# Nystrom attention with a routed FFN on one core: the pseudo-inverse's second four heads in tiles of their own, the last four batches solved in pairs

## The chip, the core and the metric

The kernel runs on one core of one Trainium2 chip. The metric is device time in microseconds of one execution; three executions of the kernel before took 290.11, 291.2 and 293.77 us, median 291.2.

The engines are named as in the profile: PE is TensorE (matrix products; PEld are its weight loads), DVE is VectorE, ACT is ScalarE, POOL is GpSimd, and SP issues most DMAs.

## What is computed

Attention by landmarks for 8 batches, 8 heads, 576 rows, 64 columns, then a mixture of experts on its output. In short:

```python
q_lm = q.reshape(B, H, 32, 18, 64).mean(3)        # 32 landmarks a head; k_lm alike
A  = softmax(scale * q @ k_lm.T)                  # 576 x 32
Bm = softmax(scale * q_lm @ k_lm.T)               # 32 x 32
C  = softmax(scale * q_lm @ k.T)                  # 32 x 576
Z = Bm.T / (norm1(Bm) * norminf(Bm) + 1e-6)
for _ in range(6):
    Z = 2 * Z - Z @ Bm @ Z                        # the pseudo-inverse
x = A @ Z @ C @ v                                 # (4608, 512) when the heads stand side by side
e = argmax(x @ w_gate)                            # one of 8 experts a row
out = p_e * sigmoid(x @ w_output_gate)[e] * (relu(x @ w1[e]) @ w2[e])
```

w1 is 8 x 512 x 1024, w2 is 8 x 1024 x 512; p_e is the softmax of the gate at the chosen expert.

## The kernel before

One core does all 8 batches. A batch is two halves (`hf`) of four heads each; the four heads of a half stand in the four groups of 32 partitions.

*Attention of a half.* SP brings q, k and v. For batches 0 to 2 TensorE transposes q and k (L455), for the others VectorE does (L469). Landmark sums are made by VectorE (L481) or GpSimd (L483 to L487). The scores of C and A (L528) use 32 x 32 or 64 x 32 tiles of the array, where head h of the queries writes to column group h, and head h of the keys to column group h+2, so that both run in different tiles. C goes through its exponential (L550), a transpose (L558) and the product with v (L570) into `XW`, a tile that holds for each half 32 columns of B beside 64 columns of C v. A is softmaxed by VectorE, ScalarE and GpSimd (L587 to L608).

*B and the pseudo-inverse of a batch.* B's scores (L621), maximum (L627), exponential with sums (L633), normalising (L645 on ScalarE or L647 on VectorE), column sums by a product with ones (L655), their largest (L661 to L664), and the scaled negative `nx` (L670 or L672). Then comes a chain of seven steps (L685): each multiplies, for every one of the eight heads, a 32 x 32 matrix by the 32 x 96 columns of the current tile (the seventh by 64), into one PSUM bank, and two copies, one for each half, bring it back into a new tile `X` (L697; the last one is L709). Matmul of head h always uses row group h and column group h; the second half follows the first through the same four tiles. A step depends on the copies of the step before. In the trace one fp32 matmul is two instructions, so a step shows 16.

*Gate and routing.* A transpose (L715), the gate's product (L723), the logits (L734) and small work on VectorE (L753 to L796) choose one main expert for the batch; GpSimd then fetches its weights with DMAs (L364, L367), unless the batch two before had the same. x transposed is made by L816.

*FFN of a batch.* 16 `up` groups of four matmuls (L861), each followed by a relu on ScalarE or VectorE (L396, L402); then, for 5 row tiles, two `down` groups each (L878, L881), the scaling (L890, L892), and the DMA out (L902). Rows whose expert isn't the main one are handled after the loop, if there are any.

*Banks.* PSUM has two pairs of banks `S` and four banks `M`. Attention work may hold at most CAPA = 4 of the four M banks, the FFN CAPF = 3, or 4 from batch LASTF = 5 on.

*What sets the order.* No engine's order is written by hand. `Plan` collects the operations of all batches with their reads, writes, tiles, an assumed duration on each engine that can do it, and a priority (PR for attention of a batch, FR for its FFN). `Plan.run` then places one operation after another by the assumed times: the one that can begin first, or one of better priority that begins soon after (TOL, PAT, MARGIN), on the engine where it ends first, with a handicap (`shy`) for VectorE or GpSimd. For TensorE it adds SWITCH = 95 ns where the tile shape changes. The program that runs has the operations of each engine in the planned order, with semaphores for the dependencies; so a changed duration or priority changes the order everywhere.

Of the kernel before, what the change touches and what calls it, by code (L numbers as in the profile page):

```python
# [71 lines left out]
class Plan:  # L72
# [6 lines left out]
    PE_LAG = 185.0  # L79
    SWITCH = 95.0  # L80
# [4 lines left out]
    MARGIN = 0.2  # L85
    SHARE = 0.6
    TOL = 60.0
    PAT = 900.0
    PAT_PE = 150.0
# [48 lines left out]
    def run(self):  # L138
# [18 lines left out]
        while ready:  # L157
            cands = []
            for o in ready:
# [106 lines left out]
def kernel(  # L266
# [75 lines left out]
    t_AT = tag("AT", 4, [128, UP])  # L342
    t_XW = tag("XW", 2, [128, 2, m + D])
    t_X = tag("X", 4, [128, 2, m + D])
    t_sm = tag("sm", 8, [128, 64])
    t_co = tag("co", B, [128, NT])
    t_ZT = tag("ZT", 4, [128, 128])
    t_nx = tag("nx", 2, [128, 2, m])
    t_G = tag("G", 2, [128, 2, m])
    t_lg = tag("lg", 2, [128, NT, m])  # L350
    t_rt = tag("rt", 2, [128, 8, NT, E])
# [17 lines left out]
    with tc.manual_schedule():  # L369
# [37 lines left out]
        def evac(n):  # L407
            return {"ACT": 45 + 0.85 * n, "DVE": 30 + 1.08 * n}
# [10 lines left out]
        def batch(b):  # L419
            pr = PR[b]  # L420
            lms, ATs, sms, ZVp = [], [], [], []
            XW = Val(t_XW)
            P.op({"": 0}, lambda e: None, w=[XW["home"]], prio=pr)
            for hf in range(2):
# [81 lines left out]
                def l_of(lm, wide, x, h, j):  # L506
                    if wide:
                        return lm.t[j * D:(j + 1) * D, x, h * m:(h + 1) * m]
                    return lm.t[h * m:(h + 1) * m, 0, (2 * x + j) * m:(2 * x + j + 1) * m]

# [4 lines left out]
                sms.append(st)  # L515
# [63 lines left out]
                def pv_out(e, pV=pV, st=st, hf=hf):  # L579
                    if e == "ACT":  # L580
                        nc.scalar.activation(out=XW.t[:, hf, m:], in_=pV.t[:, :D], func=COPY, scale=st.t[:, 3:4])
                    else:
                        nc.vector.tensor_scalar(out=XW.t[:, hf, m:], in0=pV.t[:, :D], scalar1=st.t[:, 3:4],
                                                scalar2=None, op0=MUL)
                P.op({"ACT": 230, "DVE": 190}, pv_out, r=[pV[0], st[2]], w=[XW[f"y{hf}"]], shy={"DVE": SHYE}, prio=pr + .04)

# [25 lines left out]
            pr = PR[b] + 0.1  # L612
            pB = Val(p_M, "attn", CAPA)
            sb = Val(t_sm)

            def b_scores(e):
                for hf in range(2):
                    for h in range(HH):
                        r_ = slice(h * m, (h + 1) * m)
                        for j in range(1 if wide else 2):  # L620
                            nc.tensor.matmul(pB.t[r_, hf * m:(hf + 1) * m], lhsT=l_of(lms[hf], wide, 0, h, j),  # L621
                                             rhs=l_of(lms[hf], wide, 1, h, j), start=(j == 0), stop=(j == 1 or wide))
            P.op({"PE": 150 if wide else 250}, b_scores, recs=32 if wide else 64, r=[lms[0][0], lms[1][0]], w=[pB[0]], hold=[sb],
                 mode=(D, m) if wide else (m, m), prio=pr + .025)

            def b_max(e):
                nc.vector.tensor_reduce(sb.t[:, 0:2], pB.t[:, :2 * m].rearrange("p (a r) -> p a r", a=2), axis=X, op=MAX)  # L627
            P.op({"DVE": 130}, b_max, r=[pB[0]], w=[sb[0]], prio=pr + .025)

            def b_exp(e):  # L630
                nc.scalar.mul(sb.t[:, 2:4], sb.t[:, 0:2], -s_bm)
                for hf in range(2):
                    nc.scalar.activation(out=XW.t[:, hf, :m], in_=pB.t[:, hf * m:(hf + 1) * m], func=EXP, scale=s_bm,  # L633
                                         bias=sb.t[:, 2 + hf:3 + hf], accum_out=sb.t[:, 4 + hf:5 + hf])
            P.op({"ACT": 680}, b_exp, r=[pB[0], sb[0]], w=[XW["x0"], XW["x1"], sb[1]], prio=pr + .025)

            def b_l2(ap):
                return ap.rearrange("p (a r) -> p a r", r=1).to_broadcast([128, 2, m])

            P.op({"DVE": 60}, lambda e: nc.vector.reciprocal(sb.t[:, 6:8], sb.t[:, 4:6]), r=[sb[1]], w=[sb[2]], prio=pr + .025)  # L640

            def b_norm(e):
                if e == "ACT":
                    for hf in range(2):
                        nc.scalar.mul(XW.t[:, hf, :m], XW.t[:, hf, :m], sb.t[:, 6 + hf:7 + hf])  # L645
                else:
                    nc.vector.tensor_tensor(XW.t[:, :, :m], XW.t[:, :, :m], b_l2(sb.t[:, 6:8]), op=MUL)  # L647
            P.op({"ACT": 290, "DVE": 340}, b_norm, r=[sb[2]], w=[XW["x0"], XW["x1"]], prio=pr + .025)
            pS = Val(p_M, "attn", CAPA)

            def b_cols(e):
                for hf in range(2):
                    for h in range(HH):
                        r_ = slice(h * m, (h + 1) * m)
                        nc.tensor.matmul(pS.t[r_, hf * m:(hf + 1) * m], lhsT=ones[r_, :m], rhs=XW.t[r_, hf, :m])  # L655
            P.op({"PE": 115}, b_cols, recs=32, r=[XW["x0"], XW["x1"]], w=[pS[0]], mode=(32, 32), prio=pr + .025)
# [3 lines left out]
            def b_cc(e):  # L660
                nc.vector.tensor_scalar(out=nx.t.rearrange("p a r -> p (a r)"), in0=pS.t[:, :2 * m], scalar1=1e-6, scalar2=-1.0,  # L661
                                        op0=ADD, op1=MUL)
                nc.vector.tensor_reduce(sb.t[:, 8:10], nx.t, axis=X, op=ALU.min)
                nc.vector.reciprocal(sb.t[:, 10:12], sb.t[:, 8:10])  # L664
            P.op({"DVE": 360}, b_cc, r=[pS[0]], w=[sb[3], nx[0]], prio=pr + .025)

            def b_nx(e):
                if e == "ACT":
                    for hf in range(2):
                        nc.scalar.mul(nx.t[:, hf], XW.t[:, hf, :m], sb.t[:, 10 + hf:11 + hf])  # L670
                else:
                    nc.vector.tensor_tensor(nx.t, XW.t[:, :, :m], b_l2(sb.t[:, 10:12]), op=MUL)  # L672
            P.op({"ACT": 290, "DVE": 340}, b_nx, r=[sb[3], XW["x0"], XW["x1"]], w=[nx[0]], prio=pr + .025)


            pN = Val(p_M, "attn", CAPA)
            W = m + D
            cur = XW
            for it in range(7):
                def pinv(e, cur=cur, it=it, nx=nx, pN=pN):  # L680
                    lo = 0 if it < 6 else m
                    for hf in range(2):
                        for h in range(HH):
                            r_ = slice(h * m, (h + 1) * m)
                            nc.tensor.matmul(pN.t[r_, hf * W + lo:(hf + 1) * W], lhsT=cur.t[r_, hf, :m] if it else nx.t[r_, hf],  # L685
                                             rhs=cur.t[r_, hf, lo:], start=(it == 0 and hf == 0), stop=True, skip_group_check=True)
                nxt = Val(t_X if it < 6 else t_ZT)
                P.op({"PE": 340 if it < 6 else 240}, pinv, recs=32, r=[cur[f"{x}{hf}"] for x in "xy" for hf in range(2)] +
                     ([nx[0]] if it == 0 else []), w=[pN[0], pN[1]], hold=[nxt], mode=(32, 32), prio=pr + .05)
                if it == 6:  # L690
                    break
                for hf in range(2):
                    def step(e, it=it, nxt=nxt, hf=hf, pN=pN):
                        c = 2.0 ** (0.5 * (it - 1))
                        o, i_ = nxt.t[:, hf], pN.t[:, hf * W:(hf + 1) * W]
# [4 lines left out]
                    P.op(evac(W), step, r=[pN[hf]], w=[nxt[f"{x}{hf}"] for x in "xy"], shy={"DVE": SHYE}, prio=pr + .05)  # L700
                cur = nxt
            ZV = nxt
            zk = [ZV[0]]

            def z_out(e):
                o = ZV.t.rearrange("p (a d) -> p a d", a=2)
                i_ = pN.t[:, :2 * W].rearrange("p (a c) -> p a c", a=2)[:, :, m:]
                if e == "ACT":
                    nc.scalar.mul(o, i_, -64.0)  # L709
                else:  # L710
                    nc.vector.tensor_scalar(out=o, in0=i_, scalar1=-64.0, scalar2=None, op0=MUL)
            P.op(evac(128), z_out, r=[pN[0], pN[1]], w=zk, shy={"DVE": SHYE}, prio=pr + .05)
            pZ = Val(p_M, "attn", CAPA)
            ZT = Val(t_ZT)
            P.op({"PE": 110}, recs=2, fn=lambda e: nc.tensor.transpose(pZ.t[:, :128], in_=ZV.t, identity=I128),  # L715
# [35 lines left out]
            def route1(e):  # L751
                s = rt.t[:, 6].rearrange("p i e -> p (i e)")
                nc.vector.tensor_reduce(s[:, :NT], lg.t[:, :, :E], axis=X, op=MAX)  # L753
                nc.vector.tensor_tensor(lg.t[:, :, :E], lg.t[:, :, :E], b_e(s[:, :NT]), op=SUB)
            P.op({"DVE": 450}, route1, w=[lg[0], rt[6]], prio=pr + .06)
# [235 lines left out]
```

## Time and profile before

| | us |
|---|---|
| median of three runs | 291.2 |
| profiled execution, its time | 289.87 |
| its span (first to last instruction) | 288.2 |
| TensorE busy | 259.5 (90%) |
| VectorE busy | 174.5 (61%) |
| ScalarE busy | 176.7 (61%) |
| GpSimd busy | 126.7 (44%) |
| mean granted TensorE clock | 0.984 |

How to read it: busy time of an engine is the union of its instructions. A row of a group names line, engine, operation, output <- inputs and shapes, then busy time and mean ns of one, and the idle time before with what ended it. A row of the timeline is start, length, engine, line and how many were merged. "Start to start" is what a piece of work occupies on an engine whose instructions overlap in its pipeline. A row of the stretches gives the busy microseconds of each engine within a window.

### The profile page before, as it was taken

What the parts mean: (1) busy time and instruction counts of PE and PEld (TensorE: products, weight loads), DVE (VectorE), ACT (ScalarE), POOL (GpSimd) and SP (SyncE); (2) the same over time, 40 slices, a digit from 0 to 9 for tenths busy, and PEclk for the clock granted to TensorE, in tenths of its full rate; (3) what the DMA queues carried; (4) which work ended last, traced back from release to release, by engine and by line L of the source; (5) the groups of instructions that cost most, each with busy time, mean ns of one, the idle gap of its engine ahead of it and who ended that gap; (6) DMA issues with size and microseconds to landing.
All of it is one profiled execution on the core that took longest, in us unless ns stands there. A gap on an engine that the chain in (4) does not pass through costs nothing. (4 is left out here: it accounts for less than half of the span.)

```text
span 288.2 us, 10797 instructions
## 1 busy us (share of the span) xinstructions
PE 259.5 (90%) x4452; PEld 167.3 (58%) x4453; DVE 174.5 (61%) x400; ACT 176.7 (61%) x516; POOL 126.7 (44%) x198
## 2 busy tenths in 40 slices
PE   3977789899699999999779999999999999999990
PEld 3755456575366656566456575666457576665740
DVE  5979658896998898869777998678435000000000
ACT  3658569876446767647646667485538465564740
POOL 4058752985926567772787674112200222200000
PEclk9999999999999999999997999999999999999996
DMA  7999995999898986846973041990141979994132
GB/s 270 240 362 267 252 262 173 191 302 288 122 237 192 310 207 228 187 109 181 207 151 85 5 111 32 175 227 6 33 104 36 150 156 207 224 179 129 39 99 69
DMA packets 30501, 49.01 MB, mean 170 GB/s; under 512 B 5360, under 2 KB 21744, under 8 KB 30448
## 3 DMA queue, kind: packets, MB, share of 16 engines
q1 hardware_dynamic: 20288, 37.80, 47.5%
q0 software_dynamic: 10160, 10.49, 23.6%
q8 instruction: 36, 0.59, 0.9%
q14 instruction: 17, 0.14, 0.2%
HBM read 61.90 MB, written 9.44 MB: 247 GB/s over the span
## 5 line engine op out<-in xcount | busy, mean ns | idle before, releaser
L861 PE MATMUL M<-xT_all,w 128*128 128x288 bf16 x512 | 71.7, 287 | 0.5 <-DMA w<-in_moe_w_dram 0.4
L878 PE MATMUL M<-w,hT 128*128 128x512 bf16 x256 | 59.8, 380 | 0.4 <-DMA w<-in_moe_w_dram 0.4
L861 PEld LDWEIGHTS <-w 128*128 128x128 bf16 x512 | 47.0, 98 | 18.5 <-issue 4.1
L396 ACT ACTIVATE hT<-M 128x288 bf16<-128x288 f32 x122 | 47.7, 412 | 5.4 <-PE M L861 0.4
L878 PEld LDWEIGHTS <-hT 128*128 128x128 bf16 x256 | 23.6, 98 | 27.2 <-issue 1.2
L697 ACT ACTIVATE X<-M 128x96 f32<-128x96 f32 x96 | 18.9, 248 | 27.8 <-PE M L685 26.7
L890 ACT ACTIVATE y<-M,co 128x512 f32<-128x512 f32 (+1 forms) x31 | 19.9, 645 | 22.0 <-PE M L878 15.4
L604 POOL TENSOR_TENSOR At<-At,sm 128x576 f32<-128x576 f32 x16 | 18.5, 1157 | 28.8 <-DVE sm L602 22.8
L595 POOL TENSOR_TENSOR At<-At,sm 128x576 f32<-128x576 f32 x16 | 18.6, 1170 | 24.7 <-DVE sm L590 23.6
L528 PE MATMUL S<-Tk,lm 32*32 32x288 f32 (+1 forms) x416 | 27.2, 407 | 2.2 <-issue 1.8
L685 PE MATMUL M<-X 32*32 32x96 f32 (+1 forms) x768 | 25.7, 242 | 2.5 <-issue 2.0
L528 PE MATMUL S<-Tq,lm 32*32 32x288 f32 (+1 forms) x416 | 26.2, 403 | 0.0
L685 PEld LDWEIGHTS M<-X 32*32 32x32 f32 x768 | 15.8, 104 | 15.1 <-ACT X L697 7.5
L398 ACT CAST xT_all<-S 128x576 bf16<-128x576 f32 x32 | 19.5, 643 | 5.5 <-PE S L816 5.3
L545 DVE TENSOR_REDUCE sm<-S 128x1 f32<-128x576 f32 x16 | 11.9, 747 | 13.7 <-PE S L528 13.7
L364 POOL DMA_DIRECT2D w<-in_moe_w_dram x24 | 11.8, 497 | 19.0 <-PE M L861 5.8
L367 POOL DMA_DIRECT2D w<-in_moe_w_dram x12 | 7.1, 605 | 27.6 <-PE M L881 26.8
L528 PEld LDWEIGHTS S<-Tk,lm 32*32 32x32 f32 (+1 forms) x416 | 14.4, 104 | 7.3 <-issue 3.0
L483 POOL TENSOR_TENSOR s<-nq 128x576 f32<-128x576 f32 x12 | 17.0, 1415 | 0.2
L570 PE MATMUL M<-nv,ECT 96*32 96x64 f32 x768 | 15.0, 227 | 1.9 <-issue 1.0
L484 POOL TENSOR_TENSOR s<-s 128x256 f32<-128x256 f32 x21 | 15.3, 726 | 1.6
L570 PEld LDWEIGHTS M<-nv,ECT 96*32 96x32 f32 x768 | 12.3, 114 | 6.1 <-ACT ECT L398 1.8
(125 smaller groups left out, 455.0 us busy)
## 6 DMA issues: line engine op xcount, KB each, us to landing
nk<-in_k_dram SPq DMA_DIRECT2D x16, 576.0 KB, 6.7
nq<-in_q_dram SPq DMA_DIRECT2D x16, 576.0 KB, 7.1
nv<-in_v_dram SPq DMA_DIRECT2D x48, 192.0 KB, 6.3
w<-in_moe_w_dram POOLq DMA_DIRECT2D x16, 512.0 KB, 10.3
out_dram<-y SPq DMA_DIRECT2D x128, 64.0 KB, 2.7
w<-in_moe_w_dram POOLq DMA_DIRECT2D x16, 256.0 KB, 8.1
w<-in_moe_w_dram POOLq DMA_DIRECT2D x4, 1024.0 KB
out_dram<-y SPq DMA_DIRECT2D x32, 32.0 KB, 1.6
```

Source lines behind the costliest of these rows:

```text
L396: nc.scalar.activation(out=dst(), in_=src(), func=RELU)
L398: nc.scalar.copy(dst(), src())
L483: nc.gpsimd.tensor_tensor(s3.t, n.t[:, :9], n.t[:, 9:], op=ADD)
L528: nc.tensor.matmul(p.t[o * m:(o + 1) * m, n, :U2], lhsT=l_of(lm, wide, 0 if x == "k" else 1, h, n if wide else j), rhs=t_of(Ts[x], x, wide ...
L570: nc.tensor.matmul(pV.t[h * m:(h + 1) * m, :D], lhsT=ECT.t[:, c, o * m:(o + 1) * m], rhs=n.t[:, h, c * D:(c + 1) * D], start=(c == 0), sto ...
L595: P.op({"POOL": 1115}, lambda e, At=At, st=st: nc.gpsimd.tensor_tensor(At.t, At.t, b_l(st.t[:, 8:8 + g]), op=SUB), r=[st["ax"]], w=[At[0]] ...
L604: P.op({"POOL": 1115}, lambda e, At=At, st=st: nc.gpsimd.tensor_tensor(At.t, At.t, b_l(st.t[:, 32:32 + g]), op=MUL), r=[st["as"]], w=[At[0 ...
L685: nc.tensor.matmul(pN.t[r_, hf * W + lo:(hf + 1) * W], lhsT=cur.t[r_, hf, :m] if it else nx.t[r_, hf], rhs=cur.t[r_, hf, lo:], start=(it = ...
L697: nc.scalar.mul(o, i_, c)
L861: nc.tensor.matmul(ph.t[:, :NH], lhsT=w1.t[:, dc, fc * 128:(fc + 1) * 128], rhs=xT.t[:, dc, n * NH:(n + 1) * NH], start=(dc == 0), stop=(d ...
L878: nc.tensor.matmul(py.t, lhsT=hTs[fc].t[:, i * 128:(i + 1) * 128], rhs=w2.t[:, fc, :], **f)
L890: nc.scalar.activation(out=y.t[:, :n], in_=py.t[:, :n], func=COPY, scale=com.t[:, i:i + 1])
```

## The change

1. **Second four heads in own tiles and bank.** In a step of the pseudo-inverse, head h of the second half now writes column group h+2 (mod 4) of another PSUM bank, so that a step uses eight tiles of the array and two banks. The copies turn the partitions of the second half back by 64: one copy for the first half, two (64 partitions each) for the second. The last step ends in a tile `ZV` of its own.
2. **Pairs.** `batch(b)` is cut into `attend`, `solve` and `finish`. GROUPS solves batches 0 to 3 singly, and 4+5 and 6+7 together: B's scores, softmax, column sums and all seven steps of the two batches go in one operation each, twice as wide.
3. **Plan.** Assumed durations are set anew, leaving a tile shape now costs by shape (DRAIN), and PR, FR, SHY, SHYR, MARGIN, PAT, CAPA (3) and LASTF (3) get new values. Some tiles change in number and size (`AT` 6, `X` 3 of double width, `rt` 6 instead of 8 planes).

The plan places the operations anew: TensorE visits 42 steps of the pseudo-inverse (28 single, 14 paired) instead of 56, and changes its tile shape 178 times instead of 209. In both pairs the normalising of B and `nx` stand on VectorE. 22 copies of steps stand on VectorE, none before. The loads of q, k and v keep their order but for batches 4, 5 and 7, where some change places with their neighbours and with outgoing DMAs.

```diff
+    DRAIN = {(32, 64): 178.0, (128, 32): 140.0, (64, 32): 125.0, (32, 32): 125.0, (128, 64): 130.0}
...
-    MARGIN = 0.2
+    MARGIN = 0.02
...
-    PAT = 900.0
-    PAT_PE = 150.0
+    PAT = 750
+    PAT_PE = 100
...
-                        st = max(st, free.get(e, 0.0) + self.SWITCH)
+                        st = max(st, free.get(e, 0.0) + self.DRAIN.get(mode, self.SWITCH))
...
-    SHY = 1400.0
-    SHYE = 300.0
-    SHYR = 800.0
-    PR = [0.0, 0.8, 1.9, 3.0, 4.0, 5.0, 5.9, 6.8]
-    FR = [3.0, 4.25, 6.5, 7.25, 7.5, 7.75, 9.5, 10.5]
+    SHY = 1200
+    SHYE = 200.0
+    SHYR = 0.0
+    PR = [-0.2, 0.8, 1.9, 3, 4, 4.8, 6.0, 6.9]
+    FR = [3.25, 3.25, 5.5, 7.25, 7.5, 7.75, 8.5, 8.5]
...
-    CAPA = 4
+    GROUPS = ((0,), (1,), (2,), (3,), (4, 5), (6, 7))
+    PI0, PI1, PI2 = 40.0, 165.0, 125.0
+    CAPA = 3
...
-    LASTF = 5
+    LASTF = 3
...
-            return {"ACT": 45 + 0.85 * n, "DVE": 30 + 1.08 * n}
+            return {"ACT": 78 + 0.81 * n, "DVE": 55 + 1.035 * n}
...
-            P.op({"ACT": 290, "DVE": 340}, b_norm, r=[sb[2]], w=[XW["x0"], XW["x1"]], prio=pr + .025)
+            P.op({"ACT": 215 * U, "DVE": 500 + 70 * U}, b_norm, r=[sb[2]], w=xk, prio=pr + .025)
...
-            pN = Val(p_M, "attn", CAPA)
+            pN = [Val(p_M, "attn", CAPA) for _ in range(2)]
             W = m + D
-            cur = XW
+            parts = [(0, slice(0, 128), slice(0, 128)), (1, slice(0, D), slice(D, 128)), (1, slice(D, 128), slice(0, D))]
+            cur, ck = XW, xk + yk
             for it in range(7):
...
-                    for hf in range(2):
-                        for h in range(HH):
-                            r_ = slice(h * m, (h + 1) * m)
-                            nc.tensor.matmul(pN.t[r_, hf * W + lo:(hf + 1) * W], lhsT=cur.t[r_, hf, :m] if it else nx.t[r_, hf],
-                                             rhs=cur.t[r_, hf, lo:], start=(it == 0 and hf == 0), stop=True, skip_group_check=True)
...
+                    for i in range(nb):
+                        for hf in range(2):
+                            u = hf * nb + i
+                            for h in range(HH):
+                                r_ = slice(h * m, (h + 1) * m)
+                                o = (h + 2 * hf) % HH
+                                nc.tensor.matmul(pN[hf].t[o * m:(o + 1) * m, i * W + lo:(i + 1) * W],
+                                                 lhsT=cur.t[r_, u, :m] if it else nx.t[r_, u], rhs=cur.t[r_, u, lo:],
+                                                 start=(it == 0 and i == 0), stop=True, skip_group_check=True)
...
-        for b in range(B):
-            batch(b)
+        for bs in GROUPS:
+            XW = Val(t_XW)
+            for b in bs:
+                attend(b, bs, XW)
+            solve(bs, XW)
+            for b in bs:
+                finish(b)
```

More of the change, by code (lines that the diff above doesn't have):

```diff
@@ L514, in batch @@
                 st = Val(t_sm)
-                sms.append(st)
                 def t_of(T, x, wide, n, h, j):
@@ new lines, in b_max, with b_exp @@
+            def b_max(e):
+                nc.vector.tensor_reduce(sb.t[:, 0:U], pB.t[:, :U * m].rearrange("p (a r) -> p a r", a=U), axis=X, op=MAX)
+            P.op({"DVE": 70 + 30 * U}, b_max, r=[pB[0]], w=[sb[0]], prio=pr + .025)
+            def b_exp(e):
+                nc.scalar.mul(sb.t[:, 4:4 + U], sb.t[:, 0:U], -s_bm)
+                for u in range(U):
+                    nc.scalar.activation(out=XW.t[:, u, :m], in_=pB.t[:, u * m:(u + 1) * m], func=EXP, scale=s_bm,
+                                         bias=sb.t[:, 4 + u:5 + u], accum_out=sb.t[:, 8 + u:9 + u])
@@ L623, in batch @@
[L623 to L647, printed above, removed]
```

169 lines of the change are left out of this document (97 added, 72 removed).

## The prediction

> **What bounds the kernel now.** I read the page first, then the busy time by stretches, then the waits of TensorE, and last the timeline around single steps of the pseudo-inverse. The page's own head:
>
> ```profile
> span 288.2 us, 10797 instructions
> ...
> PE 259.5 (90%) x4452; PEld 167.3 (58%) x4453; DVE 174.5 (61%) x400; ACT 176.7 (61%) x516; POOL 126.7 (44%) x198
> ```
>
> One engine stands at 90% and no other above 61%. Where TensorE's missing tenth lies is told by the stretches (first column the stretch in us, second its length, third PE busy):
>
> ```profile
> core 0: us, PE busy (x) PEld busy (x) DVE busy (x) ACT busy (x) POOL busy (x), PEclk, DMA share, GB/s
> 0.00:57.70 57.70, 44.18 (x870) 31.94 (x872) 45.13 (x86) 38.22 (x116) 31.84 (x60) 1.00 0.93 252
> ...
> 140.00:160.00 20.00, 16.38 (x395) 11.24 (x396) 13.89 (x39) 10.39 (x35) 15.42 (x23) 0.91 0.61 132
> ...
> 220.00:280.80 60.80, 60.59 (x427) 38.10 (x424) 1.82 (x12) 36.41 (x80) 8.13 (x13) 1.00 0.72 140
> sum 280.80, PE 259.51 PEld 167.32 DVE 174.53 ACT 176.31 POOL 126.66; mean PE 43.25 PEld 27.89 DVE 29.09 ACT 29.38 POOL 21.11
> ```
>
> Up to 57.7 us, where the first `up` of the FFN begins, TensorE lacks 13.5 us: inputs and the attention chain of batches 0 and 1 set the pace there, and there is no FFN work to fill with. From 57.7 to 280.8 us it is busy 215.3 of 223.1 us. The last 61 us are FFN alone, without a gap. So after 57.7 us the end is set by the sum of TensorE's work: an occupied microsecond taken off there comes off the span, if feeding it brings no new wait. The waits of TensorE (total, times, longest) say that feeding it is cheap now:
>
> ```profile
> PE M L655 <- DVE XW L647: 2.1, 1, 2.1
> ...
> PE M L685 <- ACT X L697: 0.5, 1, 0.5
> ```
>
> The evacuation of a pseudo-inverse step has cost TensorE 0.5 us in all 56 steps; the other row, VectorE's normalising of B, comes back below.
>
> **The change part by part.** The pieces of TensorE's order, by start and length:
>
> ```profile
> 108.14 0.53 PE L685 MATMUL M<-X 32*32 32x96 f32 x16
> 108.61 0.66 PE L861 MATMUL M<-xT_all,w 128*128 128x288 bf16 x4
> 109.20 0.53 PE L685 MATMUL M<-X 32*32 32x96 f32 x14
> ...
> 110.91 0.82 PE L558 MATMUL S<-I,EC 128*96 128x128 f32 x6
> 111.66 0.53 PE L685 MATMUL M<-X 32*32 32x96 f32 x16
> 112.12 0.66 PE L861 MATMUL M<-xT_all,w 128*128 128x288 bf16 x4
> 112.72 0.88 PE L570 MATMUL M<-nv,ECT 96*32 96x64 f32 x48
> 113.52 0.42 PE L685 MATMUL M<-X 32*32 32x64 f32 x16
> 113.88 0.66 PE L861 MATMUL M<-xT_all,w 128*128 128x288 bf16 x4
> 114.38 0.29 PE L715 MATMUL M<-I,ZT 128*128 128x128 f32 x1
> ```
>
> Start to start, a step takes 108.61 - 108.14 = 0.47 us (the seventh 0.36). An `up` before a step takes 0.59, before work of its own tile shape (113.88 to 114.38) 0.50: entering another shape costs about 0.10. How much of 0.47 is streaming, and what a step's evacuation costs:
>
> ```profile
> L685 PE MATMUL M<-X 32*32 32x96 f32 x640 | 22.3, 247 | 2.5 <-issue 2.0 <-ACT X L697 0.5
> ...
> L697 ACT ACTIVATE X<-M 128x96 f32<-128x96 f32 x96 | 18.9, 248 | 27.8 <-PE M L685 26.7
> ```
>
> A step lasts 0.53 and one matmul 0.247, so the 16 matmuls start within 0.28 us. They use four diagonal tiles, four matmuls each: three gaps of 0.09 us.
>
> (a) *Own tiles.* The second four heads go to four other tiles, so a step has two matmuls per tile and one gap: two gaps, 0.18 us less, if two tiles of one row group run beside each other. The scores do just that already, keys in rotated tiles, queries in diagonal ones:
>
> ```profile
> 125.06 0.43 PE L528 MATMUL S<-Tk,lm 32*32 32x288 f32 x1
> 125.07 0.42 PE L528 MATMUL S<-Tq,lm 32*32 32x288 f32 x1
> ...
> 125.33 0.40 PE L528 MATMUL S<-Tk,lm 32*32 32x288 f32 x1
> ...
> 125.57 0.40 PE L528 MATMUL S<-Tk,lm 32*32 32x288 f32 x1
> ```
>
> Eight matmuls start per 0.24 us, key and query 0.01 apart: eight tiles, two per row group, run together. Four batches are still solved singly. Each saves 6 x 0.18 + 0.12 (64 of 96 columns in the seventh) = 1.2 us. Batches 0 and 1 lie almost wholly in the stretch that waits for other things, so I count theirs as nothing (bounds 0 and 2.4); 2 and 3 give **2.4 us**.
>
> (b) *Pairs.* Batches 4+5 and 6+7 share each step: 32 matmuls on eight tiles, four per tile, which is what one old step streams. So 14 of the 28 steps go whole, with their entry: 2 x (6 x (0.47 + 0.10) + 0.36 + 0.10) = 7.8 us. A step that stands directly beside 32 x 32 scores has no shape change; there are a few more of those in the old order. I take 0.5 off: **7.3 us**.
>
> (c) *B in pairs.* Two scorings of B and two column sums go as visits of their own (their streaming stays). A visit costs an entry (0.10) and its emptying, 0.47 less the streamed 4 x 0.09 = 0.11: 4 x 0.21 = **0.8 us**. The order of TensorE's instructions agrees: 178 changes of tile shape instead of 209. FFN, scores, value products and transposes keep their numbers.
>
> (d) *Evacuation.* A single step now has three copies out of PSUM instead of two, since the second four heads are turned back by 64 partitions; a paired step has three of 192 columns in place of four of 96.
>
> ```profile
> 139.25 0.39 ACT L697 ACTIVATE X<-M 128x96 f32<-128x96 f32 x2 [0.16 <-PE M L685]
> ```
>
> Two copies in a row take 0.39, a third about 0.14 more. It offsets most of the 0.18 us that the matmuls of a single step lose, so the chain stays as long. ScalarE and VectorE at 61% have room for it. TensorE fills with an FFN piece of 0.6 or 1.0 us between most steps: nothing counted; without cover 0.14 x 28 = 4 us.
>
> (e) *The new wait.* B's chain of a pair is twice as wide, and the normalising of B and of its negative go to VectorE in both pairs. Before, ScalarE took 13 of the 16.
>
> ```profile
> L633 ACT ACTIVATE XW<-M,sm x16: 275/282/289, 22.0 to 200.7; 128x32 f32<-128x32 f32 x16
> L633 ACT ACTIVATION_READ_ACCUMULATOR XW<-M,sm x16: 192/195/201, 22.1 to 200.8; 128x1 f32 x16
> ...
> L647 DVE TENSOR_TENSOR XW<-XW,sm x2: 1010/2092/3173, 75.5 to 149.7; 128x64 f32<-128x64 f32 x2
> L672 DVE TENSOR_TENSOR nx<-XW,sm x1: 226/226/226, 157.3 to 157.3; 128x64 f32<-128x64 f32 x1
> ```
>
> The same shape on VectorE took 0.23, 1.0 and 3.2 us (min/median/max in ns); the longest gave the 2.1 us wait of TensorE above. Between B's scores and its column sums the new order has, for 4+5, three `up`, two `down` and a transposing: about 4.3 us by the rows above (`down` near 0.9). The chain needs four exponentials (4 x 0.48 = 1.9 us), the maximum and hops (0.7), and the normalising: covered up to 1.7 us. Then some 3.3 us of cover stand before the first step, against three small VectorE instructions, hops and the other product, with a 1.4 us transpose queued between: covered to about 1 us. At 0.23 nothing is lost; at 3.2 us, 1.5 + 2.2 per pair, 7.4 in all. Of the three measured values the middle one is 1.0; twice the columns bring it towards 2, which loses 0.3 + 1. I take 1.2 per pair, **2.4 us lost**. Queued behind a late product on VectorE are the transposes of the next batch's keys and the reductions of A, which have slack as long as FFN work is there.
>
> (f) *Plan constants, tiles, bank caps.* The attention may hold three of four M banks instead of four, two of them the pseudo-inverse's; FFN may hold the fourth from batch 3 on. The loads keep their order nearly. Nothing counted; bounds in the second rival.
>
> **Sum:** 2.4 + 7.3 + 0.8 - 2.4 = 8.1, so the span goes from 288.2 to 280.1. The profiled execution's own time is 289.87, 1.67 over its span: 281.8. That execution lay 1.3 us under the median of 291.2 (runs 290.11 to 293.77), so a median near 283 would be the same result. I give **282**.
>
> **Rivals.**
> *First: two tiles of one row group don't overlap here.* Then (a) gives nothing, and a paired step streams 0.37 longer: 2 x (6 x 0.20 + 0.1) = 2.6 stay of (b). With (c) and (e): about 1 us, 288.9. The rows of the scores speak against it; for it, that there each tile holds its weights for 288 columns, here for 96, so that weights come three times as often.
> [...]
>
> *Second, the slow side: banks and copies.* During a pseudo-inverse the FFN can be left with one bank.
>
> ```profile
> L396 ACT ACTIVATE hT<-M 128x288 bf16<-128x288 f32 x122 | 47.7, 412 | 5.4 <-PE M L861 0.4
> ```
>
> A bank is held 0.66 (the `up`) + 0.41 (its relu) + a hop, 1.2 us, so one `up` per 1.2 us. If a relu also stands ahead of the step's copies, a cycle is 0.36 + 0.41 + 0.53 + hops = 1.45, against 0.30 + 0.59 of work: 0.5 us lost. With 42 steps, an average loss of 0.19 eats the whole forecast (8.1); at 0.4 it is 17 us, and the time 298. Against it: the new order puts two `up` or a `down` between most steps of the pairs, and before this wait cost 0.5 us in all.
> [...]
>
> *Third: better than forecast.* The early batches give their 2.4 us, the products on VectorE meet no GpSimd work, and the stretch from 140 to 160 us, which ran at a clock of 0.91 with 3.6 us idle, is better filled: up to 6 us more, 276 to 277.
>
> **How the numbers follow.** Forecast, 278 to 286: 0.63. First rival, 287 to 290: 0.12. Second, 287 to 300: 0.15. Third, below 278: 0.10. The likeliest case gives 282. For eight in ten I reach to 276.5 (all covers hold) and to 290 (the first rival whole, half of the second). About 2% is what a measurement here can tell from no change: below 285.4 faster, above 297 slower. Faster: nearly all of the forecast and the third, 0.70. Slower: the upper part of the second rival, 0.10. Within 2%: 0.20.
>
> **What the profile after would show.** (a) Single steps of about 0.30 us start to start. (b) 14 paired steps of about 0.47, 32 matmuls each. (c) TensorE busy about 10 us less, ending near 273 instead of 280.8. (e) The two products with 128 columns on VectorE, 0.3 to 3 us, and TensorE waiting for them 1 to 3 us in all. The forecast is wrong if starts of the second four heads lag those of the first by a whole matmul, if TensorE waits for copies of X or for `hT` by more than 5 us, if FFN runs dry before the pair's weights or routing are there, or if the stretch before the first `up` grows.

## The result, and the profile after

| | before | after |
|---|---|---|
| median (lowest to highest), us | 290.65 (289.48 to 293.77) | 280.14 (278.87 to 281.31) |
| ratio, 95% interval | | 0.9621 (0.9534 to 0.9709) |
| profiled execution, its time / its span | 289.87 / 288.2 | 280.05 / 278.4 |
| TensorE busy | 259.5 | 250.6 |

The changed kernel is faster, by 3.8% (2.9 to 4.7%). Ratios, here and below, compare the fast executions of two kernels; medians are of all executions, and a profile can be of a slow one, as that of the kernel with all batches single is (1.6% above its fastest). The head of the changed kernel's page:

```profile
span 278.4 us, 10845 instructions
...
PE 250.6 (90%) x4452; PEld 159.9 (57%) x4453; DVE 178.2 (64%) x420; ACT 179.3 (64%) x497; POOL 129.6 (47%) x204
```

The span lost 9.8 us and TensorE's busy time 8.9, with the same number of matmuls. TensorE still sets the end, at the same 90%. The busy time by stretches (start and end, length, then busy us of PE, PEld, DVE, ACT, POOL), cut at the first `up` of the FFN at 59.97 us:

```profile
core 0: us, PE busy (x) PEld busy (x) DVE busy (x) ACT busy (x) POOL busy (x), PEclk, DMA share, GB/s
0.00:59.97 59.97, 45.39 (x885) 31.12 (x887) 45.48 (x95) 38.95 (x114) 39.04 (x74) 0.96 0.91 243
59.97:100.00 40.03, 38.38 (x784) 23.01 (x782) 33.96 (x77) 28.41 (x88) 26.55 (x36) 0.97 0.98 234
100.00:140.00 40.00, 39.39 (x727) 25.60 (x726) 35.28 (x78) 29.73 (x84) 26.56 (x44) 1.00 0.70 185
140.00:160.00 20.00, 17.28 (x452) 10.95 (x451) 16.68 (x29) 10.84 (x33) 12.59 (x18) 1.00 0.68 179
160.00:220.00 60.00, 59.66 (x1273) 37.39 (x1272) 41.39 (x123) 42.45 (x119) 18.51 (x27) 1.00 0.43 90
```

Before, the first `up` began at 57.7, and the stretch ahead of it ran at a clock of 1.00. Now it is 2.3 us longer and its clock 0.96 (the last section shows where it fell); TensorE lacks 14.6 us there instead of 13.5. All of the gain is behind it, and more than all. The timeline of TensorE in the kernel after shows the steps of the pseudo-inverse (L708), first single ones, then paired ones, and the last FFN matmuls (start, length, engine, line, count):

```profile
107.38 0.39 PE L708 MATMUL M<-XW,nx 32*32 32x96 f32 x16
107.70 1.16 PE L882 MATMUL M<-xT_all,w 128*128 128x288 bf16 x8
...
112.68 0.39 PE L708 MATMUL M<-X 32*32 32x96 f32 x16
113.00 1.04 PE L899 MATMUL M<-w,hT 128*128 128x512 bf16 x4
...
200.47 0.56 PE L708 MATMUL M<-X 32*32 32x96 f32 x32
200.96 1.15 PE L882 MATMUL M<-xT_all,w 128*128 128x288 bf16 x8
202.04 0.56 PE L708 MATMUL M<-X 32*32 32x96 f32 x32
202.54 1.15 PE L882 MATMUL M<-xT_all,w 128*128 128x288 bf16 x8
...
269.48 1.06 PE L902 MATMUL M<-w,hT 128*64 128x256 bf16 x16
```

A single step occupies 0.32 us (107.38 to 107.70, 112.68 to 113.00) where it occupied 0.47. A paired step, for two batches, occupies 0.49. Two `up` follow it, the next step starts 1.57 us after the last, and no gap is left. The last FFN matmuls end at 270.54; in the kernel before they ended at 280.58:

```profile
279.52 1.06 PE L881 MATMUL M<-w,hT 128*64 128x256 bf16 x16
```

So the 9.8 us split as follows: to the first `up` +2.3; from there to the last FFN matmul 222.9 before and 210.6 after, -12.3; from there to the end of the span +0.2. Of the 12.3 us, 10.1 are busy time of TensorE (215.3 before, 205.3 after, from the stretches) and 2.2 are idle time (7.6 and 5.3). The groups of the steps (busy time and mean ns, then the idle time before) say the same of TensorE's side. Before:

```profile
L685 PE MATMUL M<-X 32*32 32x96 f32 (+1 forms) x768 | 25.7, 242 | 2.5 <-issue 2.0 <-ACT X L697 0.5
L685 PE MATMUL M<-XW,nx 32*32 32x96 f32 x128 | 4.3, 247 | 0.7 <-ACT nx L670 0.7
```

After, with the group of ScalarE's copies:

```profile
L708 PE MATMUL M<-X 32*32 32x96 f32 (+1 forms) x768 | 18.2, 247 | 0.5 <-ACT X L722 0.5
L708 PE MATMUL M<-XW,nx 32*32 32x96 f32 x128 | 3.4, 250 | 0.6 <-ACT Tq L402 0.3 <-ACT nx L689 0.2
L722 ACT ACTIVATE X<-M 64x96 f32<-64x96 f32 (+3 forms) x92 | 24.9, 271 | 14.2 <-PE M L708 11.0 <-DVE X L724 1.7
```

The same 896 instructions take 21.6 us instead of 30.0, and one of them takes as long as it did: what changed is how many run beside each other. The copies cost ScalarE 24.9 us where they cost 18.9, 22 more of them stand on VectorE, and TensorE still waits for them 0.5 us in all. The waits of TensorE after (total, times, longest):

```profile
PE M L467 <- DMA nk<-in_k_dram: 4.8, 1, 4.8
PE M L882 <- issue: 3.8, 2, 2.7
PE S L564 <- ACT EC L556: 2.9, 4, 1.3
...
PE M L708 <- ACT X L722: 0.5, 2, 0.3
```

The wait for the normalising of B, 2.1 us before, is gone from the list, and it is as long as the idle time that went. The two products (in ns, min/median/max) are now twice as wide:

```profile
L666 DVE TENSOR_TENSOR XW<-XW,sm x2: 292/778/1265, 146.0 to 194.7; 128x128 f32<-128x128 f32 x2
L691 DVE TENSOR_TENSOR nx<-XW,sm x2: 291/514/736, 151.0 to 197.7; 128x128 f32<-128x128 f32 x2
```

### The profile page after: what moved, and what is told of

Same layout as the page of the kernel before. It is cut to its first block, busy times and chain, and to the rows that moved or that the text cites. A ratio compares the mean times of both kernels' runs of the same rounds, so it can differ in the third digit from the quotient of the medians.

```text
span 278.4 us, 10845 instructions
## 1 busy us (share of the span) xinstructions
PE 250.6 (90%) x4452; PEld 159.9 (57%) x4453; DVE 178.2 (64%) x420; ACT 179.3 (64%) x497; POOL 129.6 (47%) x204
## 4 chain that ended last, share of the span: by engine, by line
PE 77%; DVE 8%; issue 4%; ACT 4%; DMA 2%; POOL 2%; SPq 0%; DVEq 0%; POOLq 0%; ACTq 0%
PE M L882 22%; PE M L899 20%; PE S L534 9%; PE M L708 5%; PE S L837 4%; PE M L576 4%; PE S L564 3%; PE M L902 3%; DMA nq<-in_q_dram 2%; PE M L755 2%; PE M L467 1%; ACT EC L556 1%; PE M L638 1%; ACT X L722 1%; DVE At L595 1%
## 5 line engine op out<-in xcount | busy, mean ns | idle before, releaser
L400 ACT ACTIVATE hT<-M 128x288 bf16<-128x288 f32 x119 | 45.9, 412 | 13.2 <-PE M L882 8.8
L722 ACT ACTIVATE X<-M 64x96 f32<-64x96 f32 (+3 forms) x92 | 24.9, 271 | 14.2 <-PE M L708 11.0
L368 POOL DMA_DIRECT2D w<-in_moe_w_dram x24 | 11.7, 495 | 37.0 <-DVE lg L758 23.8
L534 PE MATMUL S<-Tk,lm 32*32 32x288 f32 (+1 forms) x416 | 26.0, 406 | 1.0 <-ACT ECT L402 0.8
L406 DVE TENSOR_SCALAR hT<-M 128x288 bf16<-128x288 f32 x9 | 3.9, 446 | 28.9 <-PE M L882 28.9
L402 ACT CAST xT_all<-S 128x576 bf16<-128x576 f32 x31 | 18.6, 638 | 5.8 <-PE S L837 5.5
L708 PE MATMUL M<-X 32*32 32x96 f32 (+1 forms) x768 | 18.2, 247 | 0.5 <-ACT X L722 0.5
L913 DVE TENSOR_SCALAR y<-M,co 128x256 f32<-128x256 f32 (+1 forms) x11 | 6.6, 601 | 17.6 <-PE M L902 17.2
L708 PEld LDWEIGHTS M<-X 32*32 32x32 f32 x768 | 10.6, 104 | 10.5 <-ACT X L722 5.2
L551 DVE TENSOR_REDUCE sm<-S 128x1 f32<-128x576 f32 x16 | 11.9, 747 | 7.3 <-PE S L534 6.7
L564 PE MATMUL S<-I,EC 128*96 128x128 f32 x96 | 13.5, 276 | 3.0 <-ACT EC L556 2.9
```

What stands on the lines that cost most here:

```text
L400: nc.scalar.activation(out=dst(), in_=src(), func=RELU)
L402: nc.scalar.copy(dst(), src())
L534: nc.tensor.matmul(p.t[o * m:(o + 1) * m, n, :U2], lhsT=l_of(lm, wide, 0 if x == "k" else 1, h, n if wide else j), rhs=t_of(Ts[x], x, wide ...
L564: nc.tensor.transpose(pE.t[:PT, c // 3, (c % 3) * 128:(c % 3 + 1) * 128], in_=EC.t[:, c % 2, c // 2 * PT:(c // 2 + 1) * PT], identity=I128)
L708: nc.tensor.matmul(pN[hf].t[o * m:(o + 1) * m, i * W + lo:(i + 1) * W], lhsT=cur.t[r_, u, :m] if it else nx.t[r_, u], rhs=cur.t[r_, u, lo: ...
L722: nc.scalar.mul(o, i_, c)
```

## The experiments

The theory: the gain comes from TensorE's own work (own tiles and pairs), the copies are hidden, the plan's constants are neutral. The rivals: it comes from the new order; or the copies and the normalising take back a part of it. All ratios are to the kernel before on the same chip; "issue" is TensorE's idle time in which it waited for nothing shown. "Half clock" adds up, over slices of 1 us until the last matmul, what the granted clock lacked to 1.00; the kernel before has 6.5 of issue and 1.7 of half clock. Spans, TensorE's busy time, issue, clock and half clock are of each kernel's profiled execution, in us but for the clock.

| kernel | ratio (95%) | span | busy | issue | clock | half clock |
|---|---|---|---|---|---|---|
| after | 0.9621 (0.9534 to 0.9709) | 278.4 | 250.6 | 6.9 | 0.980 | 3.4 |
| e1_diagonal | 0.9872 (0.9736 to 1.0008) | 281.9 | 254.3 | 6.3 | 0.988 | 1.7 |
| e5_diagonal01 | 0.9656 (0.9573 to 0.9739) | 278.2 | 249.6 | 6.7 | 0.986 | 1.7 |
| e11_shy | 0.9717 (0.9604 to 0.9830) | 282.1 | 252.9 | 8.5 | 0.973 | 5.1 |
| e9_late_norm | 0.9794 (0.9724 to 0.9864) | 286.7 | 254.9 | 10.1 | 0.969 | 6.8 |
| e3_before_newplan | 0.9977 (0.9924 to 1.0029) | 288.3 | 260.7 | 6.6 | 0.982 | 3.4 |
| e2_single_again | 1.0085 (0.9985 to 1.0185) | 291.6 | 259.2 | 9.6 | 0.969 | 6.8 |
| e10_capa4 | 1.0080 (1.0011 to 1.0149) | 291.3 | 254.4 | 10.8 | 0.964 | 8.6 |
| e8_pair23 | 1.0165 (1.0067 to 1.0262) | 292.4 | 255.7 | 10.1 | 0.966 | 8.5 |
| e4_after_oldplan | 1.0387 (1.0223 to 1.0551) | 297.6 | 257.5 | 6.9 | 0.975 | 5.1 |

**Diagonal tiles again, order kept.** The second four heads go back to their old tiles; banks, copies, pairs and order stay.

```diff
...
-                                o = (h + 2 * hf) % HH
+                                o = h
```

> The changed kernel with the second four heads back in the diagonal tiles; banks, number of copies, pairs and the order on every engine are as in the changed kernel. Theory (tiles and pairs make the gain): a single step goes from 0.33 back to 0.47 us start to start, a paired one from 0.49 to about 0.82; 24 x 0.14 + 4 x 0.10 + 12 x 0.33 + 2 x 0.22 = 8.2 us more on TensorE, of which 1.9 belong to batches 0 and 1 and are hidden: 280.1 + 6.3 = 286.4 us. Rival (the new plan's order makes the gain): 280 to 281.

Median 285.87 us, 5.7 above the kernel after. By the ratios it is 2.5% of 290, 7.3 us. Its paired steps on TensorE:

```profile
204.17 0.86 PE L708 MATMUL M<-X 32*32 32x96 f32 x32
204.97 1.16 PE L882 MATMUL M<-xT_all,w 128*128 128x288 bf16 x8
```

A paired step takes 0.80 start to start where own tiles take 0.49. So the pairs alone would have saved little of a step's streaming. The own tiles, those of the single steps included, are worth 5.7 to 7.3 us by these figures; the intervals allow 0.3 to 4.7%, and the spans differ by 3.5 us, or 5.2 with the 1.7 us that this run lost less at half clock. The theory holds on this point, since the order is the same in both kernels.

**Diagonal tiles in batches 0 and 1 alone.**

```diff
...
-                                o = (h + 2 * hf) % HH
+                                o = (h + 2 * hf * (bs[0] > 1)) % HH
```

> The changed kernel with the second four heads back in the diagonal tiles for batches 0 and 1 alone, order on every engine as in the changed kernel. By the prediction's part (a) these 14 steps lie where TensorE waits for other things and count nothing: 279 to 281 us. Rival (every step counts): 12 x 0.14 + 2 x 0.10 = 1.9 us more, 282.

The ratio is 0.9656 against 0.9621, within both intervals, and the span 278.2 against 278.4. But this run lost 1.7 us less at half clock, which can hide as much. So the steps in the stretch that waits for inputs cost 0 to 2 us; this run does not tell the theory from the rival.

**All batches single.** Own tiles stay, the pairs go; the planner makes its own order. Run twice.

```diff
-    GROUPS = ((0,), (1,), (2,), (3,), (4, 5), (6, 7))
+    GROUPS = ((0,), (1,), (2,), (3,), (4,), (5,), (6,), (7,))
```

> The changed kernel with all eight batches solved singly; own tiles and plan constants kept, the plan orders anew (56 steps, 202 changes of tile shape on TensorE). Theory: two single steps with their entries are 2 x (0.33 + 0.10) = 0.86 against 0.49 + 0.10 of a paired one; 12 x 0.27 + 2 x 0.22 + 0.8 for B = 4.5 us more: about 284.6, if the new order brings no waits of its own. Rival (order, not pairs): 280 to 282.

> The changed kernel with all batches solved singly once more, for a second profile: the first lay at 291 us where TensorE's sum said 284.6. If the third copy in 28 more steps is behind it, TensorE's waits at steps of the pseudo-inverse for copies of X (line 722 or 724) hold most of 6 us; if it is the new order of the attention, the waits lie elsewhere.

Ratios 1.0060 (1.0002 to 1.0118) and 1.0085: no faster than before, and 10 us and more over the kernel after. Neither expectation gave that. TensorE's waits in the second one:

```profile
PE S L534 <- issue: 2.7, 2, 2.0
PE M L708 <- issue: 2.4, 1, 2.4
...
PE M L708 <- ACT X L722: 2.0, 4, 1.1
PE M L708 <- DVE X L724: 0.7, 2, 0.4
```

Its TensorE is busy 259.2 us, as long as before the change, although its steps use the same tiles as a single step of the kernel after. It waits 2.7 us for copies instead of 0.5, and its clock is lower. That a single step with three copies is harder to hide is visible, but worth only 2.2 of the 13.2 us between the two spans, not most of 6 us as the second expectation had it for the copies. Stops on nothing shown are worth 2.7 more, and half clock up to 3.4; with the 4.5 of steps and entries that were expected this is 12.8. Which part of it belongs to this one execution is not shown.

**The old kernel with the new constants.** Durations, DRAIN, PR, FR, handicaps, MARGIN, PAT and LASTF as in the change; CAPA, tiles and structure as before.

```diff
...
-    FR = [3.0, 4.25, 6.5, 7.25, 7.5, 7.75, 9.5, 10.5]
+    FR = [3.25, 3.25, 5.5, 7.25, 7.5, 7.75, 8.5, 8.5]
...
-    LASTF = 5
+    LASTF = 3
...
```

> The kernel before with the plan constants of the changed one (durations, DRAIN, PR, FR, handicaps, LASTF, MARGIN, PAT), without own tiles, pairs and the attention's lower bank cap. 56 steps of 0.47 us remain and the tile shape still changes 207 times (210 before, counted in the same way). Theory: no gain, 288 to 292 us. Rival (the plan makes the gain): 281 to 284.

0.9977 (0.9924 to 1.0029): by themselves the constants bring nothing.

**The new kernel with the old constants.** The reverse: own tiles and pairs, but old PR, FR, SHY, SHYE, SHYR, MARGIN, PAT, CAPA, LASTF and no DRAIN.

```diff
...
-    CAPA = 3
+    CAPA = 4
...
-    LASTF = 3
+    LASTF = 5
```

> The changed kernel with the old plan constants (priorities, handicaps, SWITCH, MARGIN, PAT, CAPA 4, LASTF 5) around own tiles and pairs; 42 steps, 187 changes of tile shape (181 in the changed kernel). Theory: most of the gain stays, 280 to 284 us. Rival (the plan makes the gain): 287 or more.

300.23 us, 3.9% slower than before. The theory, by which most of the gain stays, falls; the rival, by which the plan makes the gain, is not true by itself either, as the run before showed. Two waits of its TensorE:

```profile
PE S L564 <- ACT EC L556: 6.5, 10, 1.2
...
PE M L576 <- ACT ECT L402: 2.8, 3, 1.1
```

With the same steps and the old constants TensorE waits 6.5 and 2.8 us for the chain of C, instead of 2.9 and 0.8. The next two runs take single constants back.

**The bank cap alone.** Attention may again hold all four M banks.

```diff
-    CAPA = 3
+    CAPA = 4
```

> The changed kernel with the attention's cap back at four of the four M banks (CAPA 4), all other constants kept, the plan orders anew. With the old constants around own tiles and pairs the time was 300 us. Theory (the pseudo-inverse's second bank leaves the FFN too few banks when the attention may take all four): 287 to 295 us. Rival (the cap isn't it): 280 to 283.

1.0080: this one constant takes the whole gain away. The time is where the theory had it, its mechanism isn't visible: no wait names a bank. The stretches to the first `up` and to 100 us:

```profile
0.00:61.55 61.55, 45.45 (x783) 31.51 (x785) 44.66 (x89) 37.20 (x106) 35.66 (x70) 0.89 0.96 243
61.55:100.00 38.45, 31.71 (x735) 19.51 (x736) 29.71 (x62) 27.38 (x90) 26.48 (x35) 0.95 0.90 212
```

By 100 us it has run 1518 matmuls, the kernel after 1669. It lacks 16.1 and 6.7 us in these stretches where the other lacks 14.6 and 1.65, at a clock of 0.89 and 0.95 instead of 0.96 and 0.97. Over the whole run it loses 5.1 us more at half clock and 3.9 more on stops with nothing shown, of 12.9 between the spans. So the cap seems to work through the order that it makes the planner find; that the FFN runs out of banks was argued and isn't shown.

**The handicaps alone.**

```diff
-    SHY = 1200
-    SHYE = 200.0
-    SHYR = 0.0
+    SHY = 1400.0
+    SHYE = 300.0
+    SHYR = 800.0
```

> The changed kernel with the three old handicaps (SHY 1400, SHYE 300, SHYR 800, which keep copies and relus on ScalarE), all other constants kept, the plan orders anew; 116 of the 126 step copies on ScalarE instead of 104. Theory (the three copies of a step need VectorE's help, and ScalarE's queue makes the waits of the run with the old constants): 284 to 290 us, with more waits of TensorE for ScalarE. Rival: 280 to 283.

0.9717 (0.9604 to 0.9830), 1% behind the kernel after with overlapping intervals: between the two expectations, at most a small part.

**A third pair.**

```diff
-    GROUPS = ((0,), (1,), (2,), (3,), (4, 5), (6, 7))
+    GROUPS = ((0,), (1,), (2, 3), (4, 5), (6, 7))
```

> The changed kernel with batches 2 and 3 solved as a third pair (35 steps, 177 changes of tile shape); plan constants kept, the plan orders anew. By TensorE's sum 6 x 0.27 + 0.22 + 0.4 for B = 2.2 us less: 278 us, if no wait comes in. Rival (batch 2 must wait for batch 3 while little FFN work is there, or the plan constants, chosen for the other grouping, no longer fit): 281 to 286 us, with TensorE waiting more between 60 and 110 us.

295.73 us, worse than both expectations and slower than before, though seven more steps have gone. Two waits of TensorE, and its busy time from 100 to 140 us:

```profile
PE S L564 <- ACT EC L556: 8.0, 6, 4.8
PE M L576 <- issue: 7.2, 3, 3.7
```

```profile
100.00:140.00 40.00, 31.52 (x702) 18.73 (x700) 31.69 (x76) 21.46 (x58) 27.38 (x45) 0.95 0.72 190
```

TensorE lacks 8.5 us in this window, 0.6 in the kernel after. A pair needs both batches' inputs and B, so the solving of batch 2 comes later, and for this pair there isn't enough FFN work yet to fill the time. That last sentence is a reading of the order; what is shown are the two stops of 3.7 and 4.8 us, and the first of them is one of those that the last section finds at fixed instruction counts, which speaks against the reading for this part.

**The normalising made late.** Twelve small reductions on VectorE stand ahead of the normalising of B in both pairs; the order stays.

```diff
...
+                    for _ in range(LATE if nb == 2 else 0):
+                        nc.vector.tensor_reduce(lt, I128, axis=X, op=MAX)
```

> The changed kernel with twelve small reductions on VectorE (about 0.2 us each, 2.5 to 3 us together) ahead of the normalising of B in both pairs; same order on every engine. By the prediction's part (e) the cover there is about 1.7 us and the product already took 0.3 and 1.3 us, so 1 to 2.5 us show for each pair: 282 to 284.5 us. Rival (the cover is longer than was worked out): 280 to 281.

286.66 us (0.9794), 1.8% behind the kernel after, more than either expectation. The second pair on TensorE's timeline, and its wait:

```profile
198.19 1.89 PE L903 MATMUL M<-w,hT 128*128 128x512 bf16 x8
202.62 0.45 PE L678 MATMUL M<-XW,ones 32*32 32x32 f32 x32 [2.54 <-DVE XW L670]
```

The reductions took 3.79 us; the column sums waited 2.54 of them, so about 1.2 was covered. The first pair's cost no wait: TensorE had stood on "issue" for 3.0 us until 148.13 and came to its column sums only at 153.16. So the wait that the prediction named exists, and its cover is about as thin as it said; in the kernel after it isn't reached. The wait of 2.54 doesn't make up the whole 1.8% (5 us): the stops on nothing shown grew by 3.2 us, and 3.4 us more were lost at half clock.

**No turning back.** The copies of the second half stay on the partitions where the products put them in six of the seven steps, once with pairs and once single.

```diff
...
-                for hf, to, of in parts:
+                for hf, to, of in ps:
...
```

> The changed kernel without turning the partitions of the second half back after each step: it stays turned by 64 partitions after odd steps, the next step turns it back by itself, and only the last step's copies turn. So a step has two copies, as before the change, instead of three (90 copies instead of 126); tiles, banks and pairs as in the changed kernel, the plan orders anew. Theory (the third copy lengthens the chain of the single steps, above all before the FFN begins at 60 us): 277.5 to 279.5 us, the first up before 59 us. Rival (copies are hidden): 280, give or take 1 for the new order.

> The same without turning, and all batches solved singly (56 steps, 2 copies a step). The run with single steps and three copies came out at 291 us where TensorE's sum said 284.6. Theory (the third copy in 28 more steps brought those waits): 284 to 286 us. Rival (steps without pairs leave waits whatever the copies): 289 to 291.

Ratios 0.9914 (0.9849 to 0.9979) and 1.0206 (1.0106 to 1.0307). These two are not to be read for the price of the third copy. The steps are written to add onto what the bank holds (`start` is set in the first alone), and a half that changes its partitions at each step adds to another head's values, so that the pseudo-inverse of the second four heads comes out as other numbers, and with it the gate and the routing behind it: the weights fetched and the rows for other experts need not be the same. The question is left to the 0.5 us of waiting in the kernel after and the 2.7 in the single one.

## Why the prediction was right, and where it wasn't

It gave 282 (276.5 to 290), faster; measured 280.14. The two ways in which it would be seen, single steps of about 0.30 and 14 paired steps of about 0.47, are there as 0.32 and 0.49, and TensorE's busy time fell by 8.9 where about 10 was named.

(a) *Own tiles*: the mechanism was right, the size too large. A step saves 0.15, not 0.18; batches 2 and 3 are worth 12 x 0.15 and a little for the seventh steps, 1.9 to 2 instead of 2.4. To count batches 0 and 1 as nothing is not contradicted, but the run with diagonal tiles there leaves room for up to 2 us.

(b) *Pairs*: 14 steps at 0.49 instead of 0.47 give 7.3 - 12 x 0.02 = 7.1. The diagonal run shows that this term hung on (a): with a paired step of 0.80, some 4 us of it go (12 x 0.31).

(c) *B in pairs*, 0.8, was not measured by itself.

(d) *Evacuation*: hidden in the kernel after, as it said (0.5 us). That it is hidden by the order, and not by itself, shows in the single kernel, where it is 2.7.

(e) *The new wait* was the mis-sized term. It was to cost 2.4 and cost nothing: the four products took 0.29 to 1.27 us, the estimate was near 2, and the covers held. The old wait of 2.1 us, which the prediction shows and gives no gain for, went too. The late normalising shows that 2.5 us more would not have been covered.

(f) *Constants at nothing*: the step that failed, although the sum came out. Alone they bring nothing, but the new tiles and pairs bring nothing without them. One cap turns 0.962 into 1.008. What the prediction treated as independent terms is a product: TensorE's saved time counts only in an order that fills it.

With the measured sizes the terms behind the first `up` give 1.9 + 7.1 + 0.8 = 9.8, and 12.3 was gained there. The 2.1 us of the old wait make it 11.9. The clock adds about 0.5: the third rival's stretch from 140 to 160 went from 0.91 to 1.00 and lost 1.7 us less, but the stretch from 60 to 100 fell from 1.00 to 0.97 and lost 1.2 more. Against all this stand the 2.3 us by which the early stretch grew, which the prediction named as a sign that it would be wrong: its clock of 0.96 is worth up to 60 x 0.04 = 2.4.

The clock's mean over the whole span hardly differs (0.984 and 0.980), but it counts the end, behind the last FFN matmuls, where the clock is 0.63 before and 0.73 after; until the last matmul the kernel after lost 3.4 us and the kernel before 1.7.

So the span's gain of 9.8 stands near the forecast 8.1 with misses that in part cancel: a loss of 2.4 that didn't come and a gain of 2.1 that wasn't counted on one side, an early loss of 2.3 that wasn't counted and the 0.7 of (a) and (b) on the other. That is in part luck, and more so is the order: five other orders of kernels with own tiles lie at 0.972 to 1.039, so how much of the 3.8% an ordinary order would keep is not known.

*First rival* (tiles of one row group don't overlap): false, by 0.32, 0.49 and the diagonal run. *Second* (banks and copies): not in the kernel after, where a paired cycle is 1.57 us without a gap. But its size of loss is real in other orders: 10 to 20 us over the kernel after in four experiments, through waits for C's chain, stops without a named cause and a lower clock; the cycle of banks that it described was not seen. *Third*: partly, in the stretch from 140 to 160 (offset from 60 to 100) and in the products on VectorE: two of the four, 0.29 us each, met no GpSimd work, and those of 0.74 and 1.27 us stood beside GpSimd pieces of 1.16.

No kernel that was run is faster than the changed one.

## What to carry to other kernels

Here two groups of small matmuls that use one row group ran beside each other when they wrote different column groups (0.49 us for a paired step, start to start); in two banks but the same column groups, as in the diagonal run, they did not (0.80). The start-to-start time of a step says at once which it is. In a kernel whose order a planner makes, run an edit with the old constants, and the new constants without the edit, before giving either the credit: here each alone was worth nothing or less. Count TensorE's instructions to its unexplained stops: if the counts are the same in different orders, the stop belongs to the place in the program and not to the work that stands there (here 690 or 691 and 942 or 943 in three orders).

## What the runs showed of the hardware

**TensorE's stops on nothing shown came at fixed instruction counts.** They are 6.3 to 10.8 us in the kernels of the table. The queues of the page after have a row for instructions:

```profile
q8 instruction: 36, 0.59, 0.9%
```

36 packets with 0.59 MB are 16.4 KB each. TensorE has 8905 instructions shown, 247 for each packet; whose instructions a packet holds the row does not say. Stretches from the start to just before a stop count TensorE's matmuls and weight loads up to it. After, at stops that end at 28.67, 37.45, 93.67 and 146.23 us:

```profile
0.00:28.50 28.50, 19.54 (x345) 14.70 (x346) 21.60 (x40) 17.47 (x46) 18.37 (x46) 1.00 0.95 283
0.00:37.40 37.40, 25.65 (x471) 18.43 (x472) 28.04 (x51) 22.97 (x65) 24.25 (x53) 1.00 0.98 269
0.00:93.60 93.60, 77.96 (x1486) 50.34 (x1488) 74.32 (x156) 63.92 (x188) 62.06 (x104) 0.96 0.95 242
0.00:146.10 146.10, 126.67 (x2503) 82.03 (x2504) 120.72 (x257) 100.58 (x300) 95.18 (x157) 0.98 0.88 227
```

Before, at stops that end at 31.26, 38.73, 144.23 and 151.54:

```profile
0.00:31.20 31.20, 20.55 (x344) 15.80 (x346) 25.59 (x41) 17.63 (x46) 14.70 (x38) 1.00 0.97 282
0.00:38.70 38.70, 26.81 (x470) 20.24 (x472) 30.47 (x48) 22.74 (x65) 19.04 (x44) 1.00 0.99 277
0.00:144.10 144.10, 125.19 (x2502) 83.28 (x2504) 117.84 (x238) 93.79 (x289) 87.82 (x144) 1.00 0.90 229
0.00:151.50 151.50, 130.63 (x2630) 87.18 (x2631) 123.28 (x249) 96.92 (x301) 93.96 (x151) 1.00 0.89 225
```

The sums are 691, 943, 2974 and 5007 after, 690, 942, 5006 and 5261 before, and 691, 943 and 3220 in the kernel with a third pair. The orders are different, the counts the same: 252 to 255 apart, or near a multiple (5007 - 2974 is 8 x 254). The ten such stops of 0.25 us or more in the profiles before and after lie within 2 instructions of 943 plus or minus a multiple of 254; in the fourteen profiles of this case 79 were found, each within 15. Nine of these stops were set against the instruction queue, in slices of 0.1 us: a packet starts 2.4 to 3.2 us before each of them ends. In the longest stop of the kernel after it starts with the stop itself, here by the queues from 143.4 to 143.6 us:

```profile
q8 instruction: 1, 0.02, 33.8%
```

At the stop of 1.04 us TensorE ran some 100 instructions between the start of the packet and the stop, at those of 2.72 and 3.68 none; the last of these begins 0.9 us before its packet does. That TensorE waits for such a packet would be a reading and isn't shown: no run moved a stop by adding instructions. The DMA engines were full (a share of 0.98 to 1.11) in seven of the eight stops listed above, but nearly empty (0.05) in the 1.72 us up to 151.54 of before. What stands just ahead of such a count differs with the order, short instructions (64 scores of B in 0.88 us shortly ahead of the stop of 2.72) or long ones; whether this is a part of what the orders above differ in isn't shown either.

At 254 apart, the 8905 instructions of the kernel after have some 35 such counts. At five of them TensorE stood for 0.25 us or more, 2.72 at the longest and 6.8 in all; at the other 30 no such stop is seen.

**The clock was lost in spells of 3.4 us at half clock, or of a multiple.** In the kernel with a third pair, the stop that ended at 104.70 and what came after it:

```profile
100.90:104.70 3.80, 0.12 (x8) 0.00 (x0) 1.04 (x3) 0.68 (x1) 3.56 (x6) 1.00 1.05 240
104.70:108.50 3.80, 3.79 (x19) 2.22 (x19) 1.65 (x5) 1.56 (x6) 3.48 (x7) 0.59 0.82 237
```

After 3.7 us without a matmul the granted clock was 0.59 on average for the next 3.8 us. In slices of 1 us every such spell before the last matmul of a profile has a clock of 0.50 inside, and together with its edges it lacks 1.7 us of full clock or a multiple (3.4, once 6.8), which is 3.4 us at half speed or a multiple. The kernel after has two spells before its last matmul, both with a clock of 0.50 over 3.4 us (38.6 to 42.0 and 59.1 to 62.5 us, the first behind the stop of 1.70 us that ended at 37.45), the kernel before has one (152.9 to 156.3), behind its stop that ended at 151.54:

```profile
39.00:42.00 3.00, 3.00 (x48) 1.73 (x48) 0.42 (x1) 1.85 (x4) 0.00 (x0) 0.50 1.05 310
153.00:156.00 3.00, 3.00 (x87) 1.93 (x77) 2.41 (x6) 1.46 (x5) 2.69 (x5) 0.50 0.11 24
```

These are the early 0.96 of the kernel after and the 0.91 from 140 to 160 us of the kernel before. The length of a stop didn't decide it: a spell came behind those of 1.70 and 1.72 us, and in the kernel after the stop of 2.72 us left the clock at 1.00.

```profile
146.20:150.00 3.80, 3.77 (x54) 2.46 (x55) 2.52 (x6) 1.14 (x3) 3.56 (x5) 1.00 1.01 218
```

What decides whether a spell follows stays open. By these figures a spell adds up to 1.7 us, or 3.4 where it is double, to the stop where TensorE sets the pace: an estimate of a part of what the slower orders above lose beyond the sum of their stops.
